# Third feature block of the experts' first products as 64x64 quarters of the PE array

## The chip, the cores and the metric

The kernel runs on one core of one Trainium2 chip. The metric is the device time of one execution in microseconds (us). Three executions of the kernel before took 200.0, 201.71 and 201.93 us, so the median is 201.71 us.

The core has five engines with instruction streams of their own: PE (matrix products; PEld is its weight load), DVE and ACT (elementwise work), POOL (elementwise work and indirect transfers) and SP (here it only issues transfers). They wait for each other through semaphores.

## What is computed

An attention-like recurrence over 768 steps (4 batches, 8 heads of 40 features) gives a matrix `x` of 3072 tokens by 320 features. It goes into a layer of 8 experts: every token belongs to the expert with the largest logit, an expert keeps its 80 tokens of largest weight, and only those get an output.

```python
for e in range(E):                       # 8 experts, D = 320 features, F = 1024
    tok_idx = np.where(expert_idx == e)[0]
    ...                                  # at most capacity = 80, by gate weight
    h = np.maximum(x[tok_idx] @ w1[e], 0.0)
    out[tok_idx] = gate_w[tok_idx, None] * (h @ w2[e])
```

The change touches `x[tok_idx] @ w1[e]`, the first product, and its ReLU. Everything is float32.

## The kernel before, in words

The recurrence (a loop over chunks of 64 steps) fills the first 105 us or so, the choice of the tokens the next 25. What follows, from about 128 us on, is the part that the change rewrites.

The order of work on each engine is the order of the code: nothing is reordered by a scheduler. So what stands on PE behind a waiting product waits too.

**Gather.** L1035: POOL issues 8 indirect transfers, one for each expert e0 to e7, that bring its 80 tokens from DRAM into `xg`. After the fourth and the eighth it writes one element of two weight buffers (L184), and these writes release SP to issue the next weight loads.

**Weights.** An expert pair p (experts 2p and 2p+1) has one tile of first weights, `wt[0, p]`, laid out as 5 blocks of 128 rows by 1024 columns: two full feature blocks for each of the two experts (256 of the 320 features), and a fifth block whose rows 0 to 63 are the last 64 features of the first expert and rows 64 to 127 those of the second. `wt[1, p]` has the second weights. Pairs 0 and 1 of the first weights are there early. The others are loaded by SP (L137) from about 133 us on, 2.6 MB a tile: second weights of pairs 0 and 1, first weights of pairs 2 and 3, then, when pairs 0 and 1 have given their tiles back, second weights of pairs 2 and 3.

**Transposes.** `f_x(p)` (L1059) has PE transpose the tokens of a pair into PSUM (three transposes for an expert), DVE copies the two full feature blocks into `cx` (named `xt` in the code), and ACT copies the last 64 features into `blk[p % 2]`. That is a tile of 128 rows by 2 x 80 columns in which the first expert has rows 0 to 63 of the first 80 columns, the second rows 64 to 127 of the last 80; the other two corners hold zeros, written once early in the recurrence (L245).

**First products.** `f_h(p)` (L1082) computes the hidden features of a pair in four rounds q of 256. A round's PSUM tile `hp` is one bank, with three banks in turn. For each 128 hidden features and each half j of 64, one product of 64 output rows by 160 columns takes the fifth weight block with `blk` for both experts at once; the zeros keep the experts apart. Then 4 products of 80 columns (2 halves x 2 feature blocks) for each expert. ACT applies the ReLU to the round (L1113) and writes it to `ht`. A product here loads its weights and multiplies twice, so the trace shows four PE instructions for one product: two loads, two multiplications.

The transposes of the next pair stand on PE behind the third round (`mid`).

**Second products.** `f_o(Q)` (L1117) multiplies `ht` of two pairs by the second weights, DVE scales the result, and POOL scatters the rows to the output (L1132).

The program at its end is `f_h(0)` with the transposes of pair 1 inside, `f_h(1)` with those of pair 2, `f_o(0)`, `f_h(2)` with those of pair 3, `f_h(3)`, `f_o(1)`. Ahead of it `warmb` (L916) puts products of zeros on PE, which write to the same `hp` banks.

## Time and profile before

| | us |
|---|---|
| median of three executions | 201.71 |
| the profiled execution | 200.67 |
| its span, first to last instruction | 198.9 |
| first transposes of the tokens start on PE | 131.28 |
| second products of pairs 0 and 1 start | 153.91 |
| first products of pairs 2 and 3 start | 167.05 |
| second products of pairs 2 and 3 start | 181.02 |

The profiled execution took 1.77 us more than its span. All times in the rows are counted from the start of the span. Of the parts after 131 us the first products take 22.6 us (pairs 0 and 1, with all waits) and 14.0 us (pairs 2 and 3).

### The profile page before, as it was taken

What the parts mean: (1) busy time and instruction counts of PE and PEld (TensorE: products, weight loads), DVE (VectorE), ACT (ScalarE), POOL (GpSimd) and SP (SyncE); (2) the same over time, 40 slices, a digit from 0 to 9 for tenths busy, and PEclk for the clock granted to TensorE, in tenths of its full rate; (3) what the DMA queues carried; (4) which work ended last, traced back from release to release, by engine and by line L of the source; (5) the groups of instructions that cost most, each with busy time, mean ns of one, the idle gap of its engine ahead of it and who ended that gap; (6) DMA issues with size and microseconds to landing.
All of it is one profiled execution on the core that took longest, in us unless ns stands there. A gap on an engine that the chain in (4) does not pass through costs nothing. (4 is left out here: it accounts for less than half of the span.)

```text
span 198.9 us, 8390 instructions
## 1 busy us (share of the span) xinstructions
PE 180.3 (91%) x3539; PEld 136.6 (69%) x3539; DVE 116.3 (58%) x352; ACT 86.1 (43%) x199; POOL 102.1 (51%) x191
## 2 busy tenths in 40 slices
PE   7999799799989999999999787885899999999990
PEld 2368478688868989888886453443899546997570
DVE  7889769799997899899998877610001111000110
ACT  7488386669768577667664300000132000321000
POOL 8768767769799589879774600176000021010111
PEclk9999999999999999999999999999699999999999
DMA  4998399899997888998799997029999999940010
GB/s 146 368 387 286 78 392 310 249 257 276 327 309 212 280 252 272 301 308 256 248 323 337 299 352 331 0 76 351 324 403 421 419 419 429 423 166 3 33 36 17
DMA packets 20819, 53.08 MB, mean 267 GB/s; under 512 B 4126, under 2 KB 12126, under 8 KB 18494
## 3 DMA queue, kind: packets, MB, share of 16 engines
q1 hardware_dynamic: 19822, 50.78, 73.5%
q0 software_dynamic: 672, 1.64, 2.5%
q8 instruction: 28, 0.46, 0.9%
q10 hardware_dynamic: 288, 0.13, 0.3%
q14 instruction: 9, 0.07, 0.1%
HBM read 43.61 MB, written 9.09 MB: 265 GB/s over the span
## 5 line engine op out<-in xcount | busy, mean ns | idle before, releaser
L1132 POOL DMA_INDIRECT out<-ob,iqi x6 | 5.9, 980 | 51.7 <-DVE ob L1131 39.4
L1094 PE MATMUL hp<-cx,w 128*64 128x80 f32 x512 | 25.6, 240 | 2.9 <-issue 1.8
L1129 PE MATMUL op<-w,ht 128*16 128x160 f32 (+2 forms) x320 | 26.6, 379 | 0.0
L1094 PEld LDWEIGHTS hp<-cx,w 128*64 128x64 f32 x512 | 23.9, 143 | 3.7 <-issue 2.1
L498 POOL TENSOR_TENSOR xn<-u,rd 128x320 f32<-128x320 f32 x23 | 16.6, 723 | 12.6 <-ACT xt L556 5.1
L1113 ACT ACTIVATE ht<-hp 128x320 f32<-128x320 f32 x16 | 7.0, 437 | 36.6 <-PE hp L1094 31.3
L1131 DVE TENSOR_SCALAR ob<-op,iq 128x320 f32<-128x320 f32 (+1 forms) x7 | 3.5, 503 | 32.8 <-PE op L1129 32.8
L533 ACT COPY cb<-cs 64x328 f32<-64x328 f32 x44 | 20.6, 467 | 4.4 <-DVE cs L528 2.7
L1129 PEld LDWEIGHTS op<-w,ht 128*16 128x16 f32 (+1 forms) x320 | 14.7, 113 | 11.0 <-issue 3.1
L556 ACT COPY xt<-tp 128x384 f32<-128x384 f32 x24 | 11.4, 478 | 18.3 <-PE tp L548 18.3
L433 PEld LDWEIGHTS sps<-qk 64*64 64x64 f32 x768 | 13.5, 134 | 7.9 <-issue 1.3
L475 PE MATMUL cps<-kv,kw 128*64 128x82 f32 x352 | 17.2, 236 | 1.5 <-issue 1.1
L442 DVE TENSOR_TENSOR p<-sps,w 128x512 f32<-128x512 f32 x24 | 16.4, 682 | 3.2 <-PE sps L433 2.5
L453 PE MATMUL h<-kv,p 128*64 128x82 f32 x352 | 16.5, 235 | 1.3 <-issue 1.1
L466 PE MATMUL hib<-cb,qk 128*64 128x82 f32 x336 | 17.2, 241 | 0.4 <-issue 0.3
L1094 PE MATMUL hp<-blk,w 128*64 128x160 f32 (+1 forms) x136 | 16.2, 306 | 0.8 <-issue 0.8
L433 PE MATMUL sps<-qk 64*64 64x64 f32 x768 | 16.8, 224 | 0.1
L1035 POOL DMA_INDIRECT xg<-xd,idx x8 | 7.9, 984 | 17.0 <-DVE gi L1046 15.0
L475 PEld LDWEIGHTS cps<-kv,kw 128*64 128x64 f32 x352 | 14.4, 136 | 2.9 <-issue 2.3
L421 POOL TENSOR_TENSOR kw<-vn,w 128x256 f32<-128x256 f32 (+1 forms) x36 | 16.1, 468 | 0.0
L453 PEld LDWEIGHTS h<-kv,p 128*64 128x64 f32 x352 | 14.3, 136 | 1.7 <-issue 1.2
L466 PEld LDWEIGHTS hib<-cb,qk 128*64 128x64 f32 x336 | 13.3, 136 | 2.2 <-issue 0.9
(215 smaller groups left out, 353.5 us busy)
## 6 DMA issues: line engine op xcount, KB each, us to landing
w<-in_w SPq DMA_DIRECT2D x14, 1280.0 KB, 17.4
qk<-in_qg SPq DMA_DIRECT2D x16, 256.0 KB, 3.9
xd<-xn SPq DMA_DIRECT2D x24, 160.0 KB, 4.2
out<-zb SPq DMA_DIRECT2D x6, 640.0 KB
xn<-in_og SPq DMA_DIRECT2D x10, 320.0 KB, 5.0
vn<-in_vn SPq DMA_DIRECT2D x8, 328.0 KB
vn<-in_vn SPq DMA_DIRECT2D x8, 320.0 KB
w<-in_w SPq DMA_DIRECT2D x8, 320.0 KB, 4.2
```

The source lines that it names most:

```text
L421: P.tensor_tensor(kw[:, :, r], kn_(c)[:, gs_(i), a:b], st["w", i][:, :, T - 1:T].broadcast_to([128, 8, b - a]), ALU.mult)
L433: mm = TE.matmul(sp[64 * y:64 * y + 64, x, q], lhsT=qk[r, 1, g], rhs=qk[r, 0, g], start=True, stop=True)
L442: V.tensor_tensor(by_x(st["p", i]), sps[:, :, i % 2], by_x(st["w", i]), ALU.mult)
L453: TE.matmul(hp[64 * r:64 * r + 64, p], lhsT=pp[:, 4 * r + p], rhs=vb[c % 2][:, 8 * hb + 4 * r + p], start=True, stop=True)
L466: TE.matmul(hi[64 * r:64 * r + 64, 2 * a:2 * a + 2, y], lhsT=qk_b[c % NV][:, 0, g], rhs=cb[:, g], start=True, stop=True)
L475: mm = TE.matmul(cpv[r0:r0 + 64, p // 2], lhsT=kw[:, p], rhs=vb[c % 2][:, 8 * hb + p], start=True, stop=True)
L498: P.tensor_tensor(xn[:, i], u, rd.broadcast_to([128, 8, D]), ALU.mult)
L533: A.copy(cb[r, gs, x], cs[r, 4 * hb:4 * hb + 4].rearrange("r q y v -> r (q y) v"))
L556: A.copy(xt, tp)
L1035: P.indirect_dma_start(xg[:, e], None, xd, bass.IndirectOffsetOnAxis(ap=idx[:, e:e + 1], axis=0), bounds_check=NTOK - 1, oob_is_err=False)
L1094: TE.matmul(out, lhsT=w[:, k, c0:c0 + 64], rhs=rhs, start=start, stop=stop)
L1129: TE.matmul(o[gw * j:gw * j + m, 0:n], lhsT=hts[p][:, f, a, t0:t0 + m], rhs=w[:, a, f, n * h:n * h + n], start=(f == 0), stop=(f == 7), ti ...
```

## The change

The zeros go, and with them `blk`. The last 64 features of both experts are kept in `xt` as a fifth block of 80 columns: rows 0 to 63 are the first expert's, rows 64 to 127 the second's.

`h_quarter` computes the third feature block as products of 64 rows by 64 output rows by 80 columns: expert a uses rows 64a to 64a+63 of the array, half j its columns 64j to 64j+63, so four successive products use four different quarters. A pair needs 32 of them in place of the 16 products of 160 columns. `h_deep` has the products of the two full feature blocks, as many as before: 64 of 80 columns for a pair.

A pair is now done in two rounds s of 512 hidden features. A round's `hp` tile is two banks, one for each expert, and there are two such tiles in turn. When a round is complete, ACT applies the ReLU to the first expert's bank and DVE to the second's (`h_out`).

The order changes. Pair 0 begins with its deep products; then come the transposes of pair 1 and of pair 2; then the quarters of pair 0, which complete it, and straight behind them the quarters of pair 1, then its deep products. Pairs 2 and 3 each have their quarters first. The transposes of pair 3 stand ahead of pair 2.

```diff
-    blk = [gp.tile([128, 2, cap], F32, name=f"blk{k}") for k in range(2)]
...
-        elif k in (4, 5):
-            P.memset(blk[k - 4], 0.0)
...
-        wt_ = pb2.tile([128, 512], F32, tag="hp", name="wmb", bufs=3)
+        wt_ = pb2.tile([128, 2, 512], F32, tag="hp", name="wmb", bufs=2)
...
-    def f_x(p):
...
+    def x_pair(p):
+        xt = ck.tile([128, 5, cap], F32, tag="xt", name=f"cx{p}", bufs=3)
+        hx[p] = xt
+        if p == 0:
+            for a in range(2):
+                xp = pb.tile([128, 3, cap], F32, tag=("db", "cn")[a], name=f"xp0{a}")
+                x_one(p, a, xp)
+                V.tensor_copy(xt[:, 2 * a:2 * a + 2], xp[:, 0:2])
+                A.copy(xt[64 * a:64 * a + 64, 4], xp[0:64, 2])
+                yield
         else:
...
-    def f_h(p, mid):
...
+    def h_open(p):
+        hts[p] = ck.tile([128, 8, 2, cap], F32, tag="ht", name=f"ht{p}", bufs=4)
+        for s in range(2):
+            hp = pb2.tile([128, 2, 512], F32, tag="hp", name=f"hp{p}_{s}", bufs=2)
+            hps[p, s] = hp[:, :, 0:4 * cap].rearrange("r a (f t) -> r f a t", t=cap)
...
+    def h_deep(p, s, a, first):
+        w, hp = h_w(p), hps[p, s]
+        for f in range(4):
+            for k in range(2):
+                for j in range(2):
+                    c0 = 128 * (4 * s + f) + 64 * j
+                    TE.matmul(hp[64 * j:64 * j + 64, f, a], lhsT=w[:, 2 * a + k, c0:c0 + 64], rhs=hx[p][:, 2 * a + k],
+                              start=(first and f == 0 and k == 0), stop=(not first and f == 3 and k == 1))
+
+    def h_quarter(p, s, first):
+        w, hp = h_w(p), hps[p, s]
+        for f in range(4):
+            for j in range(2):
                 for a in range(2):
...
+                    c0 = 128 * (4 * s + f) + 64 * j
+                    r = slice(64 * a, 64 * a + 64)
+                    TE.matmul(hp[64 * j:64 * j + 64, f, a], lhsT=w[r, 4, c0:c0 + 64], rhs=hx[p][r, 4],
+                              start=(first and f == 0), stop=(not first and f == 3))
+
+    def h_out(p, s):
+        hp, ht = hps.pop((p, s)), hts[p][:, 4 * s:4 * s + 4]
+        A.activation(ht[:, :, 0], hp[:, :, 0], AF.Relu)
+        V.tensor_scalar(ht[:, :, 1], hp[:, :, 1], 0.0, None, ALU.max)
...
+    def first_pairs():
+        x0 = x_pair(0)
+        h_open(0)
+        next(x0)
+        h_deep(0, 0, 0, True)
+        next(x0)
+        h_deep(0, 1, 0, True)
+        for s in range(2):
+            h_deep(0, s, 1, True)
+        run(x_pair(1))
+        run(x_pair(2))
+        for s in range(2):
+            h_quarter(0, s, False)
+            h_out(0, s)
+        pair(1)
+
+    def pair(p):
+        h_open(p)
+        for s in range(2):
+            h_quarter(p, s, True)
+        for s in range(2):
+            for a in range(2):
+                h_deep(p, s, a, False)
+            h_out(p, s)
+
+    first_pairs()
...
     f_o(0)
-    f_h(2, lambda: run(f_x(3)))
-    f_h(3, lambda: None)
+    run(x_pair(3))
+    pair(2)
+    pair(3)
     f_o(1)
```

Two places show how PE's order moves. A row is a product (or several alike, with their count), its output and inputs and the output's shape; the bracket names what it waits for: DMASWn is a gather's semaphore, DMAHWn a weight load's, DVE_49 and Activation_49 those engines'.

The first place is PE from the end of pair 0's deep products to the first of pair 1. Before, the transposes of pair 1 stand inside pair 0, and those of pair 2 inside pair 1, 27 rows later:

```order
L1071 MATMUL xp_2859<-cst,xg 128x80 [waits DMASW2_49,PE_49]
L1071 MATMUL xp_2859<-cst,xg 128x80
L1071 MATMUL xp_2859<-cst,xg 64x80
L1071 MATMUL xp_2859<-cst,xg 128x80 [waits DMASW3_49]
L1071 MATMUL xp_2859<-cst,xg 128x80
L1071 MATMUL xp_2859<-cst,xg 64x80
L1094 MATMUL hp_3_2870<-blk_127,w_0_1925 64x160 [waits Activation_49]
L1094 MATMUL hp_3_2870<-blk_127,w_0_1925 64x160
L1094 MATMUL hp_3_2870<-cx_2777,w_0_1925 64x80 x8
```

Now, in the changed kernel, at the same place:

```order
L1060 MATMUL xp_2852<-cst,xg 128x80 [waits DMASW3_49]
L1060 MATMUL xp_2852<-cst,xg 128x80
L1060 MATMUL xp_2852<-cst,xg 64x80
L1060 MATMUL xp_2863<-cst,xg 128x80 [waits DMASW4_49,Activation_49]
L1060 MATMUL xp_2863<-cst,xg 128x80
L1060 MATMUL xp_2863<-cst,xg 64x80
L1060 MATMUL xp_2863<-cst,xg 128x80 [waits DMASW5_49]
L1060 MATMUL xp_2863<-cst,xg 128x80
L1060 MATMUL xp_2863<-cst,xg 64x80
L1106 MATMUL hp_0_2772<-cx_2774,w_0_1921 64x80 x12
L1106 MATMUL hp_0_2772<-cx_2774,w_0_1921 64x80 [waits DMAHW3_49]
L1106 MATMUL hp_0_2772<-cx_2774,w_0_1921 64x80 x3
```

The waits for the gathers of e4 and e5 (DMASW4, DMASW5) now stand ahead of every quarter of pairs 0 and 1.

The second place is PE at the border of pairs 2 and 3 in the changed kernel, and DVE there:

```order
L1096 MATMUL hp_1_3111<-cx_2862,w_2_2727 64x80 x32
L1106 MATMUL hp_0_3213<-cx_3098,w_3_2729 64x80 [waits DMAHW7_49,DVE_49]
L1106 MATMUL hp_0_3213<-cx_3098,w_3_2729 64x80 x15
L1106 MATMUL hp_1_3214<-cx_3098,w_3_2729 64x80 [waits DVE_49]
L1106 MATMUL hp_1_3214<-cx_3098,w_3_2729 64x80 x15
L1096 MATMUL hp_0_3213<-cx_3098,w_3_2729 64x80 [waits DMAHW6_49,Pool_49]
```

```order
L1112 TENSOR_SCALAR ht_3109<-hp_0_3110 128x4x80 [waits Activation_49]
L1112 TENSOR_SCALAR ht_3109<-hp_1_3111 128x4x80 [waits Activation_49]
```

A round's quarters now wait for DVE to have read the same tile two rounds earlier, and DVE's ReLU waits for ACT's of the same round.

## Rows read from the trace of the kernel before

**Rows 1.** The page: busy shares, and DMA's tenths in 40 equal slices.

```profile
PE 180.3 (91%) x3539; PEld 136.6 (69%) x3539; DVE 116.3 (58%) x352; ACT 86.1 (43%) x199; POOL 102.1 (51%) x191
...
DMA  4998399899997888998799997029999999940010
```

**Rows 2.** Stretches A:B: length, busy time and instructions per engine, clock, DMA share, GB/s.

```profile
131.28:143.49 12.21, 8.50 (x117) 7.13 (x118) 0.65 (x2) 1.31 (x4) 5.79 (x10) 0.86 0.85 279
143.64:153.91 10.27, 10.27 (x233) 9.85 (x230) 1.05 (x3) 3.06 (x9) 0.00 (x0) 1.00 1.01 409
153.91:167.05 13.14, 13.14 (x134) 6.21 (x130) 1.10 (x2) 0.44 (x1) 1.71 (x2) 1.00 1.01 423
167.05:181.02 13.97, 13.97 (x331) 13.76 (x328) 1.04 (x2) 3.50 (x9) 1.26 (x2) 1.00 0.65 271
181.02:194.80 13.78, 13.34 (x198) 8.36 (x193) 1.87 (x4) 0.44 (x1) 1.94 (x2) 1.00 0.07 26
```

**Rows 3.** Timeline of PE, pair 0: start, length, instructions, [idle before <-what ended it].

```profile
136.16 0.30 PE L1094 MATMUL hp<-blk,w 128*64 128x160 f32 x1 [0.35 <-issue]
...
139.72 0.59 PE L1094 MATMUL hp<-cx,w 128*64 128x80 f32 x9 [1.06 <-issue]
...
140.57 1.33 PE L1094 MATMUL hp<-cx,w 128*64 128x80 f32 x16
```

**Rows 4.** The gather of expert e5: its issue on POOL's timeline, and its landing.

```profile
134.82 0.96 POOL L1035 DMA_INDIRECT xg<-xd,idx  x1 [0.30 <-issue]
...
DMA to landing us min/median/max: 8.2/8.2/8.2
```

**Rows 5.** Timeline of PE, transposes of pairs 1 and 2, products of pairs 0 and 1.

```profile
144.31 0.64 PE L1071 MATMUL xp<-cst,xg 80*128 80x80 f32 x6
144.88 0.49 PE L1094 MATMUL hp<-blk,w 128*64 128x160 f32 x4
...
147.41 0.44 PE L1094 MATMUL hp<-blk,w 128*64 128x160 f32 x4
147.68 0.72 PE L1094 MATMUL hp<-cx,w 128*64 128x80 f32 x16
148.23 0.44 PE L1094 MATMUL hp<-blk,w 128*64 128x160 f32 x4
...
151.63 0.64 PE L1071 MATMUL xp<-cst,xg 80*128 80x80 f32 x6
```

**Rows 6.** Timeline of PE in the recurrence: 16 products on 64x64 quarters, and the next.

```profile
82.05 0.69 PE L433 MATMUL sps<-qk 64*64 64x64 f32 x32
82.67 0.79 PE L466 MATMUL hib<-cb,qk 128*64 128x82 f32 x16
```

**Rows 7.** Groups by form of ACT and DVE after 128 us: busy, mean ns | idle before.

```profile
L1113 ACT ACTIVATE ht<-hp 128x320 f32<-128x320 f32 x16 | 7.0, 437 | 36.6 <-PE hp L1094 31.3 <-remote 5.3
...
L1131 DVE TENSOR_SCALAR ob<-op,iq 128x320 f32<-128x320 f32 x5 | 2.8, 551 | 29.2 <-PE op L1129 29.2
```

**Rows 8.** Stretches that begin at PE's halts for "issue", columns as in Rows 2.

```profile
36.42:41.56 5.14, 4.85 (x124) 4.24 (x124) 4.13 (x12) 2.73 (x7) 3.27 (x8) 1.00 0.86 254
...
51.19:57.03 5.84, 4.88 (x123) 4.21 (x124) 5.27 (x16) 4.19 (x9) 5.66 (x11) 1.00 0.95 316
57.03:81.01 23.98, 23.49 (x627) 20.77 (x626) 21.18 (x70) 17.44 (x43) 20.11 (x47) 1.00 0.87 263
...
95.81:131.20 35.39, 31.20 (x448) 20.52 (x448) 27.58 (x95) 9.00 (x23) 14.07 (x27) 1.00 0.75 256
```

**Rows 9.** Timeline of PE at the first of these halts.

```profile
36.43 0.38 PE L453 MATMUL h<-kv,p 128*64 128x82 f32 x5 [1.14 <-issue]
```

**Rows 10.** The page's DMA queues: packets, MB, share; then the same for 34.0 to 34.5.

```profile
q8 instruction: 28, 0.46, 0.9%
...
q8 instruction: 1, 0.02, 12.3%
```

**Rows 11.** The DMA queue of instructions from 173.5 to 174.0.

```profile
q8 instruction: 1, 0.02, 12.7%
```

## What the change will do to the time: the prediction

> **What bounds the kernel now.** First the page: PE is busy for 91% of the span, and weight traffic fills the DMA engines until about 175 us [rows 1]. A mean over stages proves little, so next come the stretches [rows 2]. From 143.64 to 181.02 PE has no idle time in the first products of pairs 1 to 3 or in the second products between them: whatever shortens PE there shortens the end. [...] Last, one resource must be looked for by hand: PE's own instructions. The page's queue q8 moved 28 instruction packets, 0.46 MB, for PE's 2 x 3539 instructions, so one packet for some 253 of them [rows 1, 10]. In the recurrence PE halts for "issue" with 1.14 us idle at 36.43 [rows 9], about 2.2 us after such a packet went out between 34.0 and 34.5 [rows 10]. From one such halt to a later one it runs 248, 247 or 1253 instructions, always about a multiple of 250, and a block takes 5.14, 5.84 or 23.98 / 5 = 4.8 us [rows 8]. I read this as blocks of instructions that are fetched one ahead, with a floor under the time of a block.
>
> **The change, part by part, first as if instructions were always there.** A pair's third block takes 8 x 0.27 = 2.2 us now (147.41 to 147.68), its other products 8 x 0.55 = 4.4 us [rows 5]. In the change the 4.4 stay. 16 products on quarters are on show in the recurrence: 0.62 us from their start to the next line's, with 64 columns [rows 6]. With 80 columns they can take at most 0.62 x 80/64 = 0.78. The lower bound is 0.55: a half-array step of two products takes 0.55 / 8 = 0.069 us [rows 5], and 16 products run twice on four quarters are 8 steps. I take 0.58, near the lower end, since the 0.62 already hold the change to the next shape, and 0.15 for each new change between quarters and half arrays (bounds 0 and 0.3). A pair's third block then takes 1.16 and saves 1.04.
>
> *Pairs 0 and 1.* The gather of e0 still opens the stage at 131.28, and pair 0's deep products (4.4 us and 6 transposes) need only e0 and e1. Even with a halt as long as today's they are done by about 142. Then PE meets the transposes of pair 2. The gather of e5 is issued at 134.82 and lands 8.2 us later, at 143.02 [rows 4]; today nobody waits for it, since these transposes run at 151.63 [rows 5]. Now every quarter of pairs 0 and 1 stands behind them. So today's halt is not saved, it is covered by this wait. From 143.02: last three transposes 0.3 (six take 0.57 [rows 5]), quarters from 143.4, pair 0 complete at 144.56. Pair 1's quarters wait until DVE has read the first tile: ACT 0.44, then DVE 0.55 [rows 7], with three handovers of about 0.13 after 143.98, so until 145.4, 0.84 us of idle. Then 1.16 + 0.15 + 4.4: second products at 151.1 instead of 153.91, **2.8 less**. If the clock is at half again after that wait, as after today's, this shrinks by up to 1.7: in the rows the slow stretch ends between 140.57 and 144.31, some 3.4 us [rows 3, 5].
>
> *Second products.* 13.14 us [rows 2], unchanged: their weights arrive in the same order, and the DMA share is 0.07 after 181.
>
> *Pairs 2 and 3.* Today 13.97 [rows 2]. Minus 2 x 1.04, plus 3 changes of shape (0.45), plus the wait of pair 3's second quarter round for DVE's reading of pair 2's second tile: 0.44 + 0.55 + 0.4 less the 0.15 + 0.58 that PE has to do meanwhile, about 0.55. That is 12.9, **1.1 less**.
>
> ReLUs on DVE (8 x 0.55) lie in its idle time, as do ACT's; two zero fills on POOL go from the recurrence, where no one waited for them. Sum so far: 200.67 - 2.8 - 1.1 = 196.8, or 198.5 with the slow clock.
>
> **Now the instructions.** A quarter product is four instructions like any other, so a pair has 96 x 4 = 384 instead of 80 x 4 = 320, in less time. Today's stages run 463 instructions in 10.27 us and 659 in 13.97 [rows 2], 5.5 and 5.3 us for 250: just above the floor of 4.8 to 5.84. The change asks for 250 in some 3.5 to 4 us. The gain can be had only where a block already lies ready. How long does a block take here? From the recurrence 4.8 to 5.84. Under the weights' traffic (409 to 423 GB/s against 254 to 316 [rows 2, 8]) perhaps more. The ends can be counted: one lies at the halt of 95.81, 896 instructions follow until 131.20 [rows 8], so the next is 104 behind that, and then every 250. Today one falls 144 to 180 instructions into pairs 2 and 3, at 170 to 171, and a packet went out only after 173.5 [rows 11]; with the 2.2 us that it took in the recurrence this is 5 to 6. The trace doesn't show when it was asked for; somewhat ahead of PE would make it 6.5. I take **5.6**, between the recurrence and that; the ends are 4.8 and 6.5.
>
> By this count the ends of the changed kernel lie about 62 instructions into the run of quarters, 56 into pair 1's deep products, 50 into the second products, 24 into pair 2's quarters, 146 into its deep products, 12 into pair 3's. Pairs 0 and 1: asked for at 143.4, the next block is there at 149.0, not at 147.7 when PE needs it; the 200 instructions left take 3.4, so second products at 152.45, **1.45 less** than today. Pairs 2 and 3: first end at the stage's start, the next blocks there at 5.6 and 11.2 (PE needs them at 4.4, and 4.1 after the first), then 244 instructions or 4.2: 15.4 instead of 13.97, **1.45 more**. A slow clock after the gather's wait overlaps with the first block's wait; I add 0.2. Sum: 200.67 - 1.45 + 1.45 + 0.2 = **200.9 us**, 0.8 under the median of the runs shown, which is 1.04 above the profiled execution.
>
> **The rivals.**
>
> *Instructions are hidden.* The array's sum holds, 196.8 to 198.5, middle 197.7. For it: today's stages show no "issue" halt after 140 although they run at 5.3 to 5.5 us for 250, so the fetch here may be quicker than I think; at 4.8 us a block my own sum is 200.67 - 2.25 - 0.15 = 198.3. Against: the recurrence's halts, which stood at slower instruction rates. [...]
>
> *Slower: the fetch under weight traffic.* The place is the ends in pair 1's, pair 2's and pair 3's deep products. At 6.5 us a block the second products of pairs 0 and 1 start 0.55 earlier than today and wait 0.55 for their own block, and pairs 2 and 3 take 6.5 + 6.5 + 4.2 = 17.2, 3.2 more: 203.9. It decides above about 6.1 us a block, where the loss passes 2 us. For it: a packet that goes out 2.6 us late under this traffic, and a gather that takes 8.2 us. Against: the last packets leave when the traffic ebbs at 175 to 178.
>
> *Quarters don't run side by side.* Then the third block costs what it did and only waits and changes are new: about 201. Four quarters in the recurrence take less than half-array products of that number would [rows 6], so this is unlikely.
>
> **Numbers.** One per cent, 2.0 us, is about what a measurement here can tell from no change. Forecast, with blocks of 5.0 to 6.1 us (199 to 202.7): 0.43. Hidden: 0.32, all of it faster by over 1%. Slower: 0.22. Not side by side: 0.03, same. So faster 0.32, same 0.46, slower 0.22. The range goes from 197.1, which leaves out about a third of the hidden case, to 203.6, which leaves out some 0.1 of the slower one. The forecast's own range is 199 to 202.7.
>
> **What would show it.** In the changed trace: a wait of PE for a gather that ends near 143.0 ahead of L1106; 16 quarters in 0.55 to 0.78 us; idle PE for DVE of about 0.8 and 0.55 us ahead of the second tiles' quarters. For the forecast: three "issue" halts of 1 to 1.7 us on L1096, about 250 instructions apart. If they are missing and pairs 2 and 3 take under 13 us, the rival of hidden instructions was right; if they exceed 2 us each, the slower one. The forecast is also wrong if e5 lands much earlier, or if the deep products of pair 0 are not done by 143.

## The result and the profile after

The changed kernel took 203.56 us (median of 22 runs, 201.43 to 205.78), the kernel before beside it 201.19 us (22 runs): a ratio of 1.0107, 95% interval 1.0074 to 1.0139. So it is slower by about 2.2 us; the forecast was 200.9 us, 0.2 above the profiled execution that it was counted from, and no change.

The profiled execution of the changed kernel was the slowest of its 22 (205.78 us, span 203.9), and those of a_late, a_mid and a_e3 below are slow ones as well. Its e0 transposes begin at 134.28, 3.0 us later than before; that is not the change, since a second profile of the same kernel has them at 131.49. So stages are counted from e0's transposes. The page: busy time, and PE's clock in 40 slices (5.1 us each).

```profile
PE 176.3 (86%) x3653; PEld 135.7 (67%) x3659; DVE 119.9 (59%) x360; ACT 82.3 (40%) x191; POOL 102.2 (50%) x189
...
PEclk9999999999999999999999999998599999999998
```

PE is busy 4.0 us less than before [rows 1], yet the end comes later. The clock digits 8 and 5 stand at about 138 to 148. The stretches, columns as in [rows 2]:

```profile
134.28:142.90 8.62, 3.86 (x60) 3.02 (x60) 0.33 (x1) 0.22 (x1) 5.83 (x10) 0.91 0.78 259
142.90:148.17 5.27, 5.27 (x75) 5.10 (x75) 0.33 (x1) 0.22 (x1) 0.00 (x0) 0.50 1.02 348
148.17:158.72 10.55, 8.29 (x270) 7.75 (x271) 2.29 (x5) 2.08 (x7) 0.00 (x0) 1.00 1.01 422
158.72:171.92 13.20, 13.20 (x135) 8.06 (x130) 1.66 (x4) 0.44 (x1) 1.36 (x2) 1.00 1.01 419
171.92:186.00 14.08, 12.83 (x394) 12.11 (x392) 2.52 (x5) 1.75 (x5) 1.61 (x2) 1.00 0.50 208
```

From e0's transposes to the second products it took 24.44 us (22.63 before), the second products 13.20 (13.14), pairs 2 and 3 14.08 (13.97): in all 2.0 us more. The granted clock was 0.50 in the second row and 1.00 in the three behind it: 0.50 over 5.27 us in which PE was never idle, just behind 8.62 us in which it was busy for 3.86. PE's timeline shows what these are:

```profile
134.28 0.40 PE L1060 MATMUL xp<-cst,xg 80*128 80x80 f32 x3
...
136.53 0.43 PE L1060 MATMUL xp<-cst,xg 80*128 80x80 f32 x3
136.88 0.55 PE L1096 MATMUL hp<-cx,w 128*64 128x80 f32 x7
138.52 0.37 PE L1096 MATMUL hp<-cx,w 128*64 128x80 f32 x4 [1.08 <-issue]
...
142.90 5.34 PE L1096 MATMUL hp<-cx,w 128*64 128x80 f32 x75 [0.91 <-issue]
148.17 1.05 PE L1060 MATMUL xp<-cst,xg 80*128 80x80 f32 x12
149.15 1.34 PE L1106 MATMUL hp<-cx,w 64*64 64x80 f32 x64
...
151.32 1.34 PE L1106 MATMUL hp<-cx,w 64*64 64x80 f32 x64 [0.83 <-DVE ht L1112]
...
155.62 3.33 PE L1096 MATMUL hp<-cx,w 128*64 128x80 f32 x89 [1.43 <-issue]
...
171.92 0.64 PE L1060 MATMUL xp<-cst,xg 80*128 80x80 f32 x6
172.48 1.34 PE L1106 MATMUL hp<-cx,w 64*64 64x80 f32 x64
173.75 3.53 PE L1096 MATMUL hp<-cx,w 128*64 128x80 f32 x94
178.20 1.41 PE L1096 MATMUL hp<-cx,w 128*64 128x80 f32 x34 [0.91 <-issue]
...
180.66 0.94 PE L1106 MATMUL hp<-cx,w 64*64 64x80 f32 x32 [0.34 <-DVE ht L1112]
```

The halt put down to "issue" (PE waits for nothing that the profile shows) in pair 0 [rows 3] is there again, a handful of multiplications at a time with 1.1 us between them, until 142.90. Behind it the remaining deep products run at half clock (0.50), 75 multiplications in 5.27 us (a product is two of them, with two loads), until 148.17. In the second profile, a_same below, it is 66 in 4.39 us. The transposes of pair 2, which by the forecast had to wait for the gather of e5, find it there: e5's gather, POOL's last release, and e5's landing (issued at 137.85, so it landed at 145.75; compare [rows 4]):

```profile
137.85 0.96 POOL L1032 DMA_INDIRECT xg<-xd,idx  x1 [0.30 <-issue]
...
141.34 0.15 POOL L184 MEMSET w<- 128x1 f32 x2
...
DMA to landing us min/median/max: 7.9/7.9/7.9
```

Further down, the quarters do what was forecast (a pair's 32 products, 172.48 to 173.75 with the change of shape), PE waits 0.83 and 0.34 us for DVE, and halts 1.43 and 0.91 us for instructions.

### The profile page after: what moved, and what is told of

It reads as the page before. It is cut to its first block, busy times and chain, and to the rows that moved or that the text cites. A ratio compares the mean times of both kernels' runs of the same rounds, so it can differ in the third digit from the quotient of the medians.

```text
span 203.9 us, 8620 instructions
## 1 busy us (share of the span) xinstructions
PE 176.3 (86%) x3653; PEld 135.7 (67%) x3659; DVE 119.9 (59%) x360; ACT 82.3 (40%) x191; POOL 102.2 (50%) x189
## 5 line engine op out<-in xcount | busy, mean ns | idle before, releaser
L1096 PE MATMUL hp<-cx,w 128*64 128x80 f32 x512 | 23.0, 251 | 7.1 <-issue 6.5
L1096 PEld LDWEIGHTS hp<-cx,w 128*64 128x64 f32 x512 | 21.4, 150 | 8.5 <-issue 7.3
L1125 PEld LDWEIGHTS op<-w,ht 128*16 128x16 f32 (+1 forms) x320 | 16.6, 113 | 9.2 <-issue 3.1
L530 ACT COPY cb<-cs 64x328 f32<-64x328 f32 x44 | 20.5, 467 | 3.6 <-DVE cs L525 2.6
L553 ACT COPY xt<-tp 128x384 f32<-128x384 f32 x24 | 11.3, 477 | 22.3 <-PE tp L545 22.3
L1112 DVE TENSOR_SCALAR ht<-hp 128x320 f32<-128x320 f32 x8 | 3.8, 490 | 20.1 <-ACT ht L1111 20.1
L536 POOL TENSOR_TENSOR cg<-cs,gl 128x328 f32<-128x328 f32 x20 | 14.7, 734 | 0.2
```

The source lines that it names most:

```text
L530: A.copy(cb[r, gs, x], cs[r, 4 * hb:4 * hb + 4].rearrange("r q y v -> r (q y) v"))
L536: P.tensor_tensor(cg.rearrange("r q y v -> r (q y) v"), cs[:, 4 * hb:4 * hb + 4].rearrange("r q y v -> r (q y) v"), gl[:, c, gs_(i)].unsqu ...
L553: A.copy(xt, tp)
L1096: TE.matmul(hp[64 * j:64 * j + 64, f, a], lhsT=w[:, 2 * a + k, c0:c0 + 64], rhs=hx[p][:, 2 * a + k], start=(first and f == 0 and k == 0), ...
L1125: TE.matmul(o[gw * j:gw * j + m, 0:n], lhsT=hts[p][:, f, a, t0:t0 + m], rhs=w[:, a, f, n * h:n * h + n], start=(f == 0), stop=(f == 7), ti ...
```

## Experiments

Kernels of one letter ran together on one chip, beside the kernel before. Its median was 201.2 us in group A (the result), 196.6 in B, 200.7 in C, 196.2 in D, 201.3 in E and 202.0 in F; D and F ran on the same chip. The result and all 18 runs; the stages are in us, from the starts in their timelines:

| group, kernel | time as a multiple of the kernel before (95%) | e0 to second products | second products | pairs 2, 3 | long halt in pair 0 |
|---|---|---|---|---|---|
| A before | 1 | 22.63 | 13.14 | 13.97 | yes |
| A after | 1.011 (1.007-1.014) | 24.44 | 13.20 | 14.08 | yes |
| B a_shift | 1.024 (1.014-1.034) | 23.32 | 13.15 | 13.19 | no |
| B b_shift | 1.001 (0.997-1.005) | 16.48 | 13.33 | 14.02 | no |
| B a_late | 1.024 (1.014-1.034) | 14.79 | 17.94 | 16.64 | no |
| B a_zeros | 1.033 (1.025-1.042) | 22.95 | 13.20 | 14.56 | no |
| C a_same | 1.010 (1.002-1.018) | 23.23 | 13.20 | 14.68 | yes |
| C b_same | one run | 21.13 | 13.14 | 13.97 | yes |
| C a_mid_shift | 1.032 (1.023-1.041) | 28.15 | 13.20 | 13.43 | yes |
| C b_x2 | 1.025 (1.019-1.030) | 25.61 | 13.15 | 13.97 | yes |
| D a_early | 1.007 (1.003-1.012) | 14.80 | 14.91 | 15.99 | no |
| D b_early | 0.9945 (0.990-0.999) | 16.07 | 13.16 | 13.97 | no |
| D a_best | 1.011 (1.002-1.019) | 15.10 | 14.73 | 16.67 | no |
| D a_mid | 1.027 (1.019-1.034) | 19.82 | 13.20 | 18.35 | no |
| E a_e3 | 1.009 (1.005-1.013) | 24.29 | 13.20 | 15.16 | yes |
| E b_e3 | 1.001 (0.998-1.005) | 22.40 | 13.14 | 13.98 | yes |
| E a_mix | 1.022 (1.018-1.027) | 23.58 | 13.20 | 17.00 | yes |
| F a_half | 0.982 (0.973-0.992) | 16.36 | 13.15 | 15.83 | no |
| F b_half | 0.973 (0.964-0.981) | 17.19 | 13.27 | 13.97 | no |
| F b_same_2 | one run | 20.96 | 13.14 | 13.97 | yes |

**1. Is the halt the end of a block of instructions?** Both kernels with 126 more PE instructions ahead of e0's transposes:

```diff
-    warmb(BW0[1])
+    warmb(4 * BW0[1], 112)
...
-    warmb(BWS[0])
+    warmb(4 * BWS[0], 112)
...
-    warmb(BWS[1])
+    warmb(4 * BWS[1], 112)
```

> This is the changed kernel with its last three groups of warm products (21 products of zeros of 512 columns, two instructions each) cut into 84 products of 112 columns. Nothing else is different; the 126 added instructions move every later block end 126 instructions earlier against the work, so the end that lay 104 instructions behind e0's first transposes falls among the warm products ahead of it, where PE waits anyway.
> Theory F (the halt in pair 0 is the end of a block of instructions, and the slow clock follows from the halt): no row of 1 us or more put down to "issue" among the first 100 instructions behind e0's transposes; the next end lies some 230 behind them, at the end of pair 0's deep products, with at most one halt there. The deep products of pair 0 are done within 8 us of e0's transposes instead of 13.9 (134.28 to 148.17), PE then waits for e5 until some 11.5 us behind them, and from e0's transposes to the second products it takes 20 to 21.5 us instead of 24.4. Time 199 to 201.
> Rival G (the halt belongs to the moment: the start of the weight transfers and POOL's gather work): the same single products with about 1.1 us of idle time from 3 to 9 us behind e0's transposes, the slow clock behind them, the stage at 24 to 25 us, time 203 to 204.
> Rival H (the clock falls first, and the halts are of no weight): halts may go, but the deep products still show 64 to 75 products in over 5 us.

> This is the kernel before with the same 126 instructions more (21 warm products of 512 columns cut into 84 of 112 columns).
> Theory F: pair 0's halt of 135.5 to 139.72 goes as well, so from e0's transposes to the second products it takes 18.5 to 20.5 us instead of 22.6 (the transposes of pair 2 come late here, so they should not wait for e5); the kernel before gains 1 to 2%, as much as or more than the changed one, which has to wait for e5.
> Rival G: 22 to 23 us, no difference in time within 1%.

PE's timeline of a_shift:

```profile
133.57 3.54 PE L1096 MATMUL hp<-cx,w 128*64 128x80 f32 x96
137.04 0.64 PE L1060 MATMUL xp<-cst,xg 80*128 80x80 f32 x6
...
140.51 0.40 PE L1060 MATMUL xp<-cst,xg 80*128 80x80 f32 x3 [2.84 <-DMA xg<-xd,idx]
143.47 0.66 PE L1060 MATMUL xp<-cst,xg 80*128 80x80 f32 x3 [2.56 <-DMA xg<-xd,idx]
144.06 4.84 PE L1106 MATMUL hp<-cx,w 64*64 64x80 f32 x128
148.83 4.02 PE L1096 MATMUL hp<-cx,w 128*64 128x80 f32 x104
...
153.58 1.05 PE L1096 MATMUL hp<-cx,w 128*64 128x80 f32 x24 [0.73 <-issue]
```

There is no halt; the deep products are done 5.9 us behind e0's transposes (137.04). Then PE waits 2.84 and 2.56 us for the gathers of pair 2, and behind that wait it runs slower: 128 multiplications on quarters take 4.84 us (64 took 1.34 in the changed kernel). So the wait that the forecast counted on exists when the halt is away, and it brings the slow clock with it. The mean clock of what follows is 0.75; that of b_shift is 1.00 throughout, in 16.48 us:

```profile
144.06:154.46 10.40, 9.66 (x257) 9.08 (x258) 1.97 (x4) 1.75 (x5) 0.00 (x0) 0.75 1.01 413
...
167.61:180.80 13.19, 12.42 (x394) 11.87 (x392) 2.50 (x5) 1.75 (x5) 1.43 (x2) 1.00 0.66 272
```

```profile
131.51:147.99 16.48, 15.79 (x346) 14.92 (x348) 1.70 (x5) 4.38 (x13) 5.82 (x10) 1.00 0.89 308
```

b_shift's stage came out shorter than expected (18.5 to 20.5 us), a_shift's longer (20 to 21.5), and b_shift was no faster than the kernel before beside it. The kernel before took 196.6 us in this group, 4.6 less than in group A, and no trace of it was taken here: most likely its halt was not there to begin with, as it is in neither of the group's unshifted kernels (a_late, a_zeros). So theory F was neither shown nor refuted.

**2. Weight transfers later, and quarters with zeros** (also group B). a_late has

```diff
-        if e in (3, 7):
-            for h in held[e // 4 * 2:e // 4 * 2 + 2]:
+        if e == 7:
+            for h in held:
```

> This is the changed kernel with POOL's four releases of the held weight loads put behind all eight gathers (in the changed kernel, two stand behind the fourth). The weight transfers begin later, so gathers and the block of instructions that PE needs in pair 0 meet less traffic.
> Theory F with a fetch that is slowed by the traffic: the halt in pair 0 (137.2 to 142.9 in the changed kernel's profile) shrinks to under 2 us, e5 lands within 8 us of e0's transposes (11.5 in the changed kernel), pair 0's start to the second products 19 to 21.5 us instead of 24.4; what comes later may wait for the later weights, by at most the 2 us by which they start later.
> If the fetch does not feel the traffic (a rival within F): the halt stays 5 to 6 us long, and the stage at 23 to 25 us. Rival G says that the halt goes with POOL's gather work, so it stays too, perhaps earlier.

The gathers land in 2.7 us (median; e5's took 7.9 in the changed kernel), PE waits for none, and the first stage takes 14.79 us. But the second products wait for their weights (2.13 and 1.73 us in two rows, more than the 2 us expected), and pairs 2 and 3 take 16.64 with halts of 1.58 and 1.89 us. What the early stage gained, the transfers took back.

a_zeros has

```diff
-                    r = slice(64 * a, 64 * a + 64)
-                    TE.matmul(hp[64 * j:64 * j + 64, f, a], lhsT=w[r, 4, c0:c0 + 64], rhs=hx[p][r, 4],
+                    TE.matmul(hp[64 * j:64 * j + 64, f, a], lhsT=w[:, 4, c0:c0 + 64], rhs=blk[p % 3][:, a],
```

> This is the changed kernel with the third block's 64x64 quarters computed as products of 128 rows with zeros in the other expert's rows, in the same order and the same number (32 for a pair, 80 columns). They use half arrays, so the array needs more time for them; the instructions stay as many. 32 half-array products are 2.2 us by the kernel before where quarters are some 1.2.
> If PE is bound by the array in pairs 1 to 3, each pair gets about 1 us longer: 3 to 4 us in all, 1.5 to 2% more time.
> If it is bound by the supply of instructions (the prediction's step for pairs 2 and 3), pairs 2 and 3 together stay at 14.1 us within 0.6, because their halts of 0.9 to 1.5 us shrink by what the array takes more; in pairs 0 and 1 at most 1 us more.

Pairs 2 and 3 take 14.56 us, against 14.08 and 14.68 with quarters in the two profiles of the changed kernel. Each pair's third block needs some 1 us more of the array (2.27 us in pair 2, 168.31 to 170.58, against 1.27), and the stage did not get longer by it: its halt shrank to 0.21 us. So in those two profiles the halts, and not the array, set the length of pairs 2 and 3. They don't everywhere: a_shift, in the same group, takes 13.19 us with quarters, 0.8 less than the kernel before, with one halt of 0.77:

```profile
174.02 0.78 PE L1106 MATMUL hp<-cx,w 64*64 64x80 f32 x31
175.56 0.83 PE L1106 MATMUL hp<-cx,w 64*64 64x80 f32 x33 [0.77 <-issue]
```

The place of these halts is that of the ends of blocks. In the changed kernel PE halts behind 6 + 64 + 94 = 164 multiplications of the stage (178.20), and a_early below halts there and 127 later (254 instructions with their loads), behind 291. In a_shift, whose stream is 126 instructions or 63 multiplications further on, it halts behind 6 + 64 + 128 + 31 = 229, where 291 - 63 = 228.

**3. The same two kernels on another chip, and pair 2's transposes alone.**

> The changed kernel once more, with no edit, on the chip of the runs beside it, since on the chip of the first four experiments the kernel before took 196.62 us and not 201.19. If the halt in pair 0 is there in every run, the stage from e0's transposes to the second products is 24 to 25 us again and pairs 2 and 3 take 14.1. If the halt comes only in some executions, then without it PE has to wait for e5 as it did with the shifted blocks, and the stage is 23 to 23.5. Both theories: 1 to 2.5% slower than the kernel before on the same chip.

> The kernel before once more, with no edit, for its trace on this chip. With the shifted blocks it was no faster than without (196.2 against 196.62 us), though its first stage was 16.5 us where the profile of the kernel before has 22.6. If pair 0's halt is a thing of some chips or some executions, this profile may show none and 16.5 us; if it is always there, it shows 22 to 23 us again, and the time that the shift gained has been lost at another place.

Both halt, until 8.5 us behind e0's transposes, and the changed kernel again needs more: 2.1 us in the first stage, 0.7 in pairs 2 and 3. Stretches of a_same and of b_same, halt and what follows:

```profile
131.49:139.97 8.48, 5.00 (x70) 3.42 (x69) 0.33 (x1) 0.22 (x1) 5.77 (x10) 0.82 0.79 259
139.97:144.36 4.39, 4.39 (x66) 4.17 (x67) 0.32 (x1) 0.22 (x1) 0.00 (x0) 0.56 1.01 325
```

```profile
131.81:140.30 8.49, 4.89 (x65) 2.98 (x64) 0.65 (x2) 0.44 (x2) 5.77 (x10) 1.00 0.78 259
140.30:143.35 3.05, 3.05 (x72) 2.96 (x72) 0.00 (x0) 0.88 (x2) 0.00 (x0) 1.00 0.98 320
```

Busy time in the halt is alike (5.00 and 4.89 us), but in a_same the clock fell (0.82, then 0.56), in b_same it did not. The halt does not always bring the slow clock.

a_mid_shift moves pair 2's transposes in the shifted changed kernel, b_x2 moves them in the shifted kernel before:

```diff
         run(x_pair(1))
-        run(x_pair(2))
...
         pair(1)
+        run(x_pair(2))
```

```diff
-    f_h(1, lambda: run(f_x(2)))
+    run(f_x(2))
+    f_h(1, lambda: None)
```

> The changed kernel with the blocks of instructions shifted by 126, and with pair 2's transposes moved from before pair 0's quarters to behind pair 1. So nothing in pairs 0 and 1 waits for the gathers of e4 and e5.
> Theory F2 (the change loses because its new order makes PE wait for e5, some 12 us behind e0's transposes, and because the clock is at half for some us after that wait; its products themselves are faster): no wait on a gather and no slow clock, from e0's transposes to the second products 14.6 to 16 us (23.3 with the early transposes, 16.5 in the kernel before with the same shift), pairs 2 and 3 13 to 14.1 us, time 1 to 3% under the kernel with the early transposes and up to 1.5% under the kernel before with the shift. Second products cannot begin before their weights are there, about 14 us behind e0's transposes.
> Rival S (the drained accumulators and the supply of instructions cost what the quarters save): 16.5 us or more, no faster than the kernel before.

> The kernel before, with the blocks of instructions shifted by 126, and with one piece of the change alone: pair 2's transposes are put ahead of pair 1's products (they stand behind pair 1's third round otherwise). No quarters, no other accumulators.
> Theory F2: PE waits for e5 some 3 to 4 us, the clock falls, and the stage takes 19 to 22.5 us in place of 16.5; the time is 1.5 to 3% over that of the shifted kernel before.
> Rival S: the order is of no weight, 16.5 to 17.5 us.

Both miss. On this chip the shift did not remove the halt, it moved it to e0's transposes and made it 8 us long. a_mid_shift, PE, then DVE, then POOL's last release:

```profile
131.92 0.30 PE L1060 MATMUL xp<-cst,xg 80*128 80x80 f32 x2 [0.21 <-issue]
140.30 2.40 PE L1096 MATMUL hp<-cx,w 128*64 128x80 f32 x32 [8.08 <-DVE cx L1069]
```

```profile
139.92 0.33 DVE L1069 COPY cx<-xp 128x160 f32<-128x160 f32 x1 [9.25 <-remote]
```

```profile
138.45 0.15 POOL L184 MEMSET w<- 128x1 f32 x2
```

PE's third transpose starts at 131.99, but DVE's copy of its result starts at 139.92. The idle time moved with the shift, if not by the full 126 instructions (in the unshifted profiles that halt it begins 85 to 110 instructions behind the start of e0's transposes, 60 in b_e3 below; here 6), so the place in the instruction stream counts. Its end did not move with it: 139.92 is 1.33 us behind the release (138.45 + 0.15). The changed kernel unshifted holds a result back in the same way: e1's transposes start at 136.53 (above), and DVE copies them only when the halt is over:

```profile
143.01 0.33 DVE L1069 COPY cx<-xp 128x160 f32<-128x160 f32 x1 [7.80 <-remote]
```

In a_early below, which has no such halt, the two times are 133.12 and 133.58. A block of instructions that comes late does not by itself explain that a transpose already started is handed over so late. The wait for e5 was hidden by the halt in both kernels, so what the order alone costs was not tested here.

**4. Weights early, gathers alone** (group D). In both kernels the first half of pair 0's second weights is sent early, the rest behind all gathers:

```diff
-    held = [load_w(wq, 1, 0, held=(0,)), load_w(wq, 1, 1, held=(0,))]
+    held = [load_w(wq, 1, 0, held=(1,)), load_w(wq, 1, 1, held=(0,))]
...
+    run(held[0], 1)
...
-        if e in (3, 7):
-            for h in held[e // 4 * 2:e // 4 * 2 + 2]:
+        if e == 7:
+            for h in held:
```

> The changed kernel with another start of the weight transfers. The first half of the second weights of pair 0 (1.28 MB) is no longer held: it goes out behind the traffic before it, into the 10 us in which the DMA engines are idle (124 to 134). All the others are released behind the eighth gather (before: half of them behind the fourth). So the gathers and the end of the block of instructions in pair 0 meet no weight traffic, and the second products need not wait for their weights as with the late release.
> Theory F2 (gathers and the fetch of instructions both suffer from the weight transfers that start among the gathers; PE's idle time there and the slow clock behind it are what the change loses on): e5 lands within 9 us of e0's transposes, no halt of over 2 us in pair 0, no slow clock, 14.5 to 16 us from e0's transposes to the second products (23 to 24.5 in the changed kernel), 13.2 for the second products, 13.2 to 16.6 for pairs 2 and 3 (with the late release their two halts made it 16.6). From e0's transposes to the last second products 42 to 45.5 us where it was 49.7 to 51.7; 2 to 4% under the kernel before.
> Rival P (chance decides where PE halts): a halt of 4 to 8 us in pairs 0 or 1 all the same.

> The kernel before with the same other start of the weight transfers (half of pair 0's second weights early, the others behind the eighth gather). Theory F2: no long halt in pair 0 and no slow clock, 16 to 17 us from e0's transposes to the second products, 13.2, and 14.0 for pairs 2 and 3: 43.2 to 44.2 in all. Against the changed kernel with the same start this tells what the products of the change are worth by themselves: 2 x 1.04 us and more for it if only the array counts (42 or less against 43.7), nothing or a loss if the supply of instructions takes back what the quarters save (43 to 45.5 against 43.7).

a_early was expected 2 to 4% under the kernel before and is 0.7% over it; b_early's stages came as expected. This is the cleanest comparison of the two kernels: no halt in pair 0, no wait for a gather, clock 1.00. The changed products win 1.27 us in pairs 0 and 1 (14.80 against 16.07) and lose 2.02 in pairs 2 and 3 (15.99 against 13.97); the second products take 1.75 more, 1.04 of it in one wait for weights. Timeline of a_early:

```profile
151.89 8.92 PE L1126 MATMUL op<-w,ht 128*64 128x320 f32 x94 [1.04 <-DMA w<-in_w]
...
167.31 1.41 PE L1097 MATMUL hp<-cx,w 128*64 128x80 f32 x34 [1.20 <-issue]
168.65 0.78 PE L1107 MATMUL hp<-cx,w 64*64 64x80 f32 x32
169.77 0.78 PE L1107 MATMUL hp<-cx,w 64*64 64x80 f32 x32 [0.34 <-DVE ht L1113]
170.49 1.25 PE L1097 MATMUL hp<-cx,w 128*64 128x80 f32 x29
...
173.35 3.61 PE L1097 MATMUL hp<-cx,w 128*64 128x80 f32 x98 [1.61 <-issue]
```

Two halts, 1.20 and 1.61 us. Between their ends (167.31 and 173.35) lie 34 + 32 + 32 + 29 = 127 multiplications, 254 instructions with their loads, and 6.04 us. Pairs 2 and 3 of a_early, then of b_early:

```profile
160.75:176.74 15.99, 12.84 (x394) 12.02 (x392) 2.50 (x5) 1.75 (x5) 1.03 (x2) 1.00 0.92 382
```

```profile
130.99:147.06 16.07, 15.65 (x347) 14.82 (x348) 1.70 (x5) 4.37 (x13) 5.72 (x10) 1.00 0.66 235
...
160.22:174.19 13.97, 13.97 (x331) 13.76 (x328) 1.04 (x2) 3.49 (x9) 1.39 (x2) 1.00 1.01 421
```

b_early runs the same stage with no idle time under at least as much traffic (DMA share 1.01 against 0.92), 659 instructions in 13.97 us, 5.4 for 254: a rate that the supply followed. b_early is 0.5% faster than the kernel before (0.990 to 0.999); the changed kernel itself did not run in this group.

a_best puts the second round's quarters between the deep products:

```diff
-        for s in range(2):
+        h_quarter(p, 0, True)
+        for s in range(2):
+            if s == 1:
                 h_quarter(p, s, True)
-        for s in range(2):
```

> The changed kernel with that start of the weight transfers, and with the quarters of a pair's second round put between its two rounds of deep products instead of ahead of both (pairs 1 to 3). Then DVE has read the accumulators before PE wants them again (the idle times of 0.83 and 0.34 us ahead of L1106 go), for two more changes of shape, some 0.3 us, in a pair. If PE waited only for DVE there: 0.5 us less in pairs 0 and 1. If the supply of instructions is the bound: the halts grow by what the waits lose, and the time stays within 0.5 us of that without this edit.

The 0.34 us went, the first round's 0.83 stayed, the halts became 1.67 and 1.66: no gain, as expected if the supply is the bound.

> The changed kernel with one edit: pair 2's transposes stand behind pair 1's products instead of ahead of pair 0's quarters, so no product of pairs 0 and 1 stands behind the gathers of e4 and e5. The weight transfers start as in the changed kernel.
> Theory F2, on a chip where pair 0 halts: the halt ends some 8.5 us behind e0's transposes, later work is no longer waiting for e5 anyway, and the stage stays at 22.5 to 24.5 us. On a chip where it doesn't halt: no wait for e5, no slow clock, 14.6 to 16 us instead of 23.3, and the kernel is 2 to 4% faster than the changed one.
> Rival S (the array and the accumulators): no difference in either case.

a_mid (the order edit of a_mid_shift without the shift) expected 14.6 to 16 us and took 19.82. The wait for e5 is gone, and a new halt takes its place, with slow products behind it, 83 multiplications in 4.77 us where the changed kernel has 89 in 3.33 (155.62):

```profile
147.23 4.77 PE L1096 MATMUL hp<-cx,w 128*64 128x80 f32 x83 [2.89 <-issue]
```

It falls where the changed kernel halts for 1.43 us (155.62) and a_half below, under weight traffic, for 1.35; a_early and a_late, whose gathers meet no weights, have no halt there. So theory F2 was too simple: with the weights among the gathers the next block seems to come late as well. The 18.35 us of pairs 2 and 3 hold two halts (1.66 and 1.83) and a second slow stretch (97 multiplications in 5.25 us behind the second halt, where a_early has 98 in 3.61; the clock is 0.91 in the mean).

**5. More weights early, and fewer instructions** (group E).

```diff
-    held = [load_w(wq, 1, 0, held=(1,)), ...
+    held = [load_w(wq, 1, 0, 4, held=(3,)), ...
...
-    run(held[0], 1)
+    run(held[0], 3)
```

> The changed kernel with three quarters (1.92 MB) of pair 0's second weights sent early and the rest behind the eighth gather (a_early: one half). Theory F2: pairs 0 and 1 take 14.8 us again, the second products find their weights and take 13.2 to 13.5 us (14.9 with one half early), pairs 2 and 3 16 us with two halts of 1.2 to 1.7 us: 44 to 44.5 us from e0's transposes to the last second products, within 0.5% of b_e3's time or up to 1% above it. Rival: the transfer that goes out at 124 to 129 delays the first gathers, and e0's transposes come 1 us or more later than 131.

> The kernel before with the same early three quarters. 16.1, 13.2 and 14.0 us, 43.2 in all, as with one half early (its second products did not wait there): no difference to b_early, so 0.5% under the kernel before on a chip on which its pair 0 doesn't halt, and 2 to 3% under it on a chip on which it does.

> a_e3 with pairs 2 and 3 computed as in the kernel before: third block with zeros for both experts at once, 80 products for a pair instead of 96, ReLU on ACT, transposes of pair 3 inside pair 2; pairs 0 and 1 keep the quarters. If the number of instructions is what makes pairs 2 and 3 slower in the changed kernel, they take 14.0 us without a halt of over 0.5 us, and the whole is 14.8 + 13.2 + 14.0 = 42.0 us: 1.2 less than b_e3, 2 less than a_e3, the fastest of all, 0.5 to 1% under b_e3. If it is something else in the changed kernel (its accumulators, its clock), pairs 2 and 3 stay at 15 to 16 us.

All three miss: they halt in pair 0, with no weight transfer between e0's transposes and POOL's last release (the gathers land in 3.6 us in a_e3); in b_e3 the halt begins already at e1's transposes (PE waits 3.50 us for DVE, until 137.00). So the transfers are not what makes PE halt there: F2 falls on this point too. The early start brought no gain here (b_e3 1.001). In a_mix no "issue" row is left in pairs 2 and 3, which fits the count of instructions, but its accumulators, two rounds to a tile, made PE wait 4 x 0.54 us for ACT, so the stage took 17.00 and tells nothing of the gain.

**6. Half of the gathers** (group F). What all halts so far but one had in common was their end, 1.2 to 1.4 us behind POOL's last gather and release (in b_e3 the long idle time was over at 137.00, ahead of the release at 137.97). So the last four gathers were taken out:

```diff
-        P.indirect_dma_start(xg[:, e], None, xd, ...
+        if e < 4:
+            P.indirect_dma_start(xg[:, e], None, xd, ...
...
-            TE.transpose(xp[0:n, k], xg[:, e, 128 * k:128 * k + n], ident[0:cap, 0:cap])
+            TE.transpose(xp[0:n, k], xg[:, e % 4, 128 * k:128 * k + n], ident[0:cap, 0:cap])
```

> The changed kernel without the gathers of e4 to e7; pairs 2 and 3 work on the tokens of pairs 0 and 1. PE has the same instructions, POOL's gathers end 5 us earlier, and the four releases of the weights follow each other at 133 to 134.
> Theory G2 (PE halts as long as POOL issues gathers): on a chip that halts, the halt in pair 0 ends by 1.5 us behind the last release, some 4 us behind e0's transposes instead of 8.5; the deep products end within 9 us of e0's transposes (12.9 and 13.9 in the two profiles of the changed kernel that halt). On a chip that doesn't halt there is no wait for e5, so in both cases 15 to 19 us from e0's transposes to the second products instead of 23.2 to 24.4.
> Theory F (the halt lasts by itself, as a fetch does): it ends some 8.5 us behind e0's transposes as before, 22 us and more.

> The kernel before without the gathers of e4 to e7; pairs 2 and 3 work on the tokens of pairs 0 and 1. Theory G2, on a chip that halts: the halt ends some 4 us behind e0's transposes instead of 8.5, the stage takes 16.5 to 18.5 us instead of 21.1 to 22.6, and the time is 2% or more under that of the kernel before. Theory F: 21 us and more, no difference. On a chip that doesn't halt: 16 to 16.5 us, no difference.

> The kernel before with no edit, for its trace on this chip: 21 to 23 us from e0's transposes to the second products with a halt that ends 1.2 to 1.4 us behind POOL's last release, or 16 to 16.5 us without one.

The kernel before halts on this chip until 139.12, 1.27 us behind the release. PE, then POOL:

```profile
139.12 0.51 PE L1094 MATMUL hp<-cx,w 128*64 128x80 f32 x8 [0.50 <-issue]
```

```profile
137.70 0.15 POOL L184 MEMSET w<- 128x1 f32 x2
```

Without the four gathers neither kernel has a halt in pair 0, though PE has the same instructions at the same places. First stage and pairs 2 and 3 of a_half, first stage of b_half:

```profile
133.59:149.95 16.36, 13.77 (x404) 12.75 (x404) 2.93 (x7) 2.52 (x9) 1.84 (x6) 1.00 0.89 347
...
163.10:178.93 15.83, 13.18 (x394) 12.30 (x391) 2.50 (x5) 1.75 (x5) 1.96 (x2) 1.00 0.82 341
```

```profile
131.72:148.91 17.19, 16.24 (x346) 14.81 (x347) 1.70 (x5) 4.37 (x13) 1.91 (x6) 1.00 0.89 349
```

The clock is 1.00. b_half is 2.7% faster than the kernel before (0.964 to 0.981), and a_half, the changed kernel without the gathers, 1.8% faster than the kernel before (0.973 to 0.992); the changed kernel itself did not run in this group. The changed products again win 0.83 us in pairs 0 and 1 and lose 1.86 in pairs 2 and 3, so without the halt the change still loses, to halts for instructions (0.93 and 1.38 us in pairs 2 and 3). G2 holds in this: in this group the halt needs the last four gathers. The weights are released earlier with these gathers gone, so it is not that pair 0 meets the weight transfers later.

Three things in the traces narrow the cause down. First, the halt lies about where a block of instructions ends: in 15 of the 16 unshifted profiles, halt or none, the next packet of PE's instructions [rows 10] goes out 104 to 138 instructions behind e0's first transpose (277 in b_half), in the changed kernel between 142.3 and 142.6, in a_early between 134.2 and 134.5. In a_half that place comes 3.5 us behind e0's transposes, when POOL's loop has been over for 1.3 us. Second, the end goes with POOL's issuing and not with the gathers' landing: in the changed kernel the halt is over at 142.90, before e5 lands (145.75), and in a_e3, where gathers land in 3.6 us, it ends 1.24 us behind the last release, against 1.41. Third, the issuing is not enough: in groups B and D POOL issues its eight gathers in the same rhythm, 1.27 us apart, and PE does not halt. This is not the chip: the kernel before took 194.4 to 198.9 us in D and 200.8 to 204.2 in F, on the same one. What differs stays open.

## Why the prediction was wrong

**What failed.** The step "even with a halt as long as today's they are done by about 142", and its conclusion that the halt "is not saved, it is covered by this wait"; the term is the clock's price, put at 0.2 us. The halt was as long as today's [rows 3]: it ended 8.6 us behind e0's transposes, 8.4 before. The 75 multiplications left behind it would have taken 2.7 us at full clock (96 take 3.47 in a_shift, 133.57 to 137.04), so pair 0's deep products would have been done 11.3 us behind e0's transposes, just ahead of e5's landing at 11.5, and the step would have held. But they ran at half clock (0.50) and took 5.27 us, 2.6 too much, until 13.9 us behind e0's transposes. That is the prediction's own sign of being wrong: deep products not done by 143, 11.7 us behind. I had read the half clock behind today's halt (0.50 in the kernel before from 140.57 to 143.49; 16 products in 1.33 us against 0.72), but charged it to the time behind e5's wait, where I let it overlap with a later wait for instructions (0.2, at most 1.7). So the first stage, forecast at 21.4 us (22.63 less 1.45, plus 0.2 for the clock), took 24.44 us, in the second profile 23.23. Of the 3.0 us, 2.75 lie ahead of the quarters (14.87 us behind e0's transposes, forecast 12.1), the rest behind; in the second profile 1.7 of 1.8 (13.85). What makes PE halt there, and why the clock fell in a_same and not in b_same, stays open.

In the sum, the term of pairs 0 and 1 (1.45 less) came out as 1.8 more (2.1 in group C), and that of pairs 2 and 3 (1.45 more) as 0.1 more (0.7). That the whole is off by no more than 2 us is partly luck: the two errors have opposite signs.

**A halt that is not there would not have saved it.** In a_shift PE waits for e5, the clock falls too (0.75), and the stage takes 23.32 us against 16.48 in b_shift, whose transposes of pair 2 come late enough not to wait. So with its own start of the weight transfers the changed kernel loses this stage either way: 6.8 us there, 1.8 and 2.1 where both halt. Where the gathers meet no weights, or there are only four, it wins it by 1.27 and 0.83 (a_early, a_half).

**Right.** e5's landing (11.5 us behind e0's transposes, 11.7 forecast); quarters side by side, 1.27 for a run of 32 with the change of shape (1.31); DVE's first wait, 0.83 (0.84); second products unchanged; two of the three halts for instructions on L1096, in pair 1 and pair 2 (1.43 and 0.91 us, 1.25 and 1.30 in the second profile), none in pair 3. DVE's second wait was 0.34 us where the prediction has 0.55; the terms that it gives add up to 0.66.

**Right in mechanism, wrong in size.** Pairs 2 and 3: forecast 15.4, measured 14.08 and 14.68, but 15.83 and 15.99 in a_half and a_early, where the weights flow through most of the stage (DMA share 0.82 and 0.92; 0.50 in the changed kernel's profile). The block's time of 5.6 us was somewhat short under traffic (6.04 between two halts) and too long where the traffic ebbs: in the changed kernel's profile the block end of pair 3 brings no halt. Where the ends fall counts as well: a_shift needs 13.19 us at a DMA share of 0.66. What a block's end costs differed from stage to stage: 1.20 and 1.61 us in a_early's dense short products, nothing in b_early, at a lower rate (254 instructions in 5.4 us; in a_early in 4.4, the 6.04 between its halts' ends less the second halt).

**The rivals.** None came as described. "Hidden" is refuted by the halts in pairs 1 and 2, "not side by side" by the 1.27 us of a pair's quarters, where half arrays need 2.27 in a_zeros. The slower rival gave nearly the right time (203.9) by luck: it is 3.2 us more than the execution that it was counted from, where the measured loss is 2.2, and it put the loss into pairs 2 and 3, where it arose in pair 0.

## What to carry to other kernels

Before counting a wait as covered by another, ask what ends each, and at which clock the work between them runs: idle PE time here was often, though not in b_same, paid twice, by the idle and by the lower clock behind it (0.50 over 5.27 us in the changed kernel, 1.00 in b_same). Moving a consumer of a gather ahead of work that does not need it is safe only if the gather lands before that work would be done without any halt (in a_shift the work was done 5.9 us behind e0's transposes, and PE waited 2.84 and 2.56 us). Where an edit trades few long products for many short ones, compare instructions per us with what the supply has been seen to deliver (254 in 5.4 us in b_early); the array's gain (1.27 us in pairs 0 and 1 of a_early, whose pairs 2 and 3 lose 2.02 with halts of 1.20 and 1.61) stays only where instructions and weights are already there.

## What was not expected of the hardware

- PE halts for 4 to 8 us while POOL issues indirect gathers: in nine of ten profiles that halt, from four groups, the halt ends 1.2 to 1.4 us behind POOL's last release, and with four gathers instead of eight it is absent. In two groups it is absent with eight.
- In such a halt a transpose that PE began at 131.99 reached DVE only at 139.92 (a_mid_shift), in the changed kernel one of 136.53 only at 143.01.
- Halts at the ends of blocks lie 254 instructions apart in the traces and move with the stream (a_early, a_shift); 254 instructions in 5.4 us ran without a halt (b_early), the denser stages of the change halted at such ends for 0.8 to 1.9 us, though not at each.
- The same halt left the clock at 1.00 in b_same and at 0.56 over the following products in a_same, with 4.89 and 5.00 us of busy time in 8.5.
- A gather of 80 rows lands in 2.7 us with no weight transfers beside it in a_late (median; 3.6 in a_e3), and in 7.9 with them (e5 in the changed kernel).
